# A two-layer Fourier and attention kernel: late Fourier matmuls and early score maxima as 64-row pairs, with one key tile

## The chip, the cores and the metric

The kernel runs on one core of one Trainium2 chip. The metric is the device time of one execution in microseconds. PE is TensorE (PEld its weight loads), DVE VectorE, ACT ScalarE, POOL GpSimd, SP SyncE, which issues most DMAs. A matmul's result goes to PSUM, which has eight banks of 512 fp32 columns on 128 partitions.

## The reference, cut to what matters

```python
def _A_ref(x, dft_seq_re, dft_seq_im, dft_hid_re, dft_hid_im):
    a = jnp.einsum("bsd,ed->bse", x, dft_hid_re)
    b = jnp.einsum("bsd,ed->bse", x, dft_hid_im)
    return jnp.einsum("ts,bse->bte", dft_seq_re, a) - jnp.einsum("ts,bse->bte", dft_seq_im, b)

def _B_ref(x, wq, wk, wv, wo):          # 32 query heads of 16, one key and one value head
    q = (x @ wq).reshape(B, S, H, Dh).transpose(0, 2, 1, 3)
    k, v = x @ wk, x @ wv
    p = softmax(jnp.einsum("bhqd,bkd->bhqk", q, k) * Dh ** -0.5)
    o = jnp.einsum("bhqk,bkd->bhqd", p, v)
    return o.transpose(0, 2, 1, 3).reshape(B, S, H * Dh) @ wo

x = x + _A_ref(layernorm(x), ...)       # S = 2048, D = 512
x = x + _B_ref(layernorm(x), ...)
x = x + _A_ref(layernorm(x), ...)
x = x + _B_ref(layernorm(x), ...)
```

## The kernel before

Each of the two layers has a Fourier stage (`phase_a`) and an attention stage (`phase_b`). All instructions are issued in an order written out by hand; each engine takes its own in that order. Products are made of two-part fp32r numbers, a high part `...h` and a low part `...l`: `mm3` (L87) issues high x high, high x low and low x high into the same PSUM bank.

**Fourier stage.** The output rows are in four blocks `tb` of 512. For each block the sequence transform comes first, once with the cosine matrix (c = 0) and once with the sine matrix (c = 1): a loop over n = 0..127, with `tb, c, s = n // 32, (n // 16) % 2, n % 16`, takes one chunk of 128 rows of the matrix, split into `ch` and `cl`. For each of the four column tiles d it adds `xnh`/`xnl` chunk s times the chunk into `z[d]`: twelve 128-row matmuls of 512 columns a chunk. The four banks of z are two two-bank tiles `x` (`pair()`, bufs 2). Chunks 112 to 127 (c = 1 of block 3) are worked in two halves of 256 columns. After the sixteenth chunk `z_split` (ACT, DVE and POOL) empties z into `zh[c]`, `zl[c]`. After c = 1 the hidden transform follows: `y_tile` for each of four row tiles, 24 matmuls into one bank `y`, then on DVE the residual add and the statistics of the next normalization, and a DMA to `mid`.

During block tb + 1, `prep_tasks` prepares block tb: normalization, four transposes, `kv` (n = 32 (tb + 1) + 6), v's transposes and four projections `q_mm` (+7 to +10), each into a bank `y`, and their stores to `qd` in DRAM. For block 3 that work stands behind the loop (the tail).

**Maxima.** The softmax needs each row's maximum over all keys. For some (query tile i, key block kb) this is done already in the Fourier stage: `EARLY` lists them with the query tile's slot, when to load it and between which times the 32 maxima are spread. Times there count 40 to a block, 32 chunks and 8 for y. Each is one matmul into a bank `y` (bufs 3) and one `reduce_max` on DVE. PE, DVE and the three banks are all that couples them to the rest.

The head pairs lie on the two halves of the partitions: rows 0 to 63 hold head g = 0, rows 64 to 127 head g = 1 of a pair `pr`. `kz[g]` holds the keys on half g and zeros on the other half, so the early maximum of one head takes all 128 rows of the query tile:

```python
def max_one(i, pr, g, c0, n, to):
    pm = bank("y")[:, :n]
    nc.tensor.matmul(pm, o.qT[i][:, pr, :], kz[g][:, c0:c0 + n], start=True, stop=True)
    nc.vector.reduce_max(to, pm, axis=AX.X)
```

The maxima and scores of the attention stage (`max_half` L354, `score` L739) use 64 rows of one half already, two heads after one another on different halves.

**Attention stage.** For each of 16 query tiles and 32 steps it makes the scores of four heads, ACT's exponentials, and the products with v. The change leaves its instructions as they are but for the name of the key tile.

`hl_tiles` gives four buffers each for `ch` and `cl`, which the query weights share (`wq_split`). `qd_zero` writes zeros from `kz[0]` into the spare rows of `qd` in DRAM, a task each at n = 20 + 2 t in layer 0, from POOL's queue.

Of the kernel before, what the change touches and what calls it, by code (L numbers as in the profile page):

```python
# [17 lines left out]
P = 128  # L18
S = 2048
# [22 lines left out]
]  # L42
KEPT = [e for e in EARLY if e[0]]
# [5 lines left out]
def fnet_mqa_kernel(ctx: ExitStack, tc: tile.TileContext, x_in, ct, dt_, wq, wkv, wo, out):  # L49
# [66 lines left out]
    def qd_zero(t):  # L116
        for g in range(2):
            nc.gpsimd.dma_start(qd[t, 64 * g + M0:64 * g + 64, :], f(kz[0][64:64 + 64 - M0, :]))
# [4 lines left out]
    def hl_tiles():  # L123
        return (sb.tile([P, 512], F32R, name="ch", bufs=4), sb.tile([P, 512], F32R, name="cl", bufs=4))
# [63 lines left out]
    def make_layer(L, src, mid, dst, last):  # L188
# [68 lines left out]
        def kv(t0, n, xth, xtl, vt=None, now=True):  # L257
# [15 lines left out]
        def kv_lo(t0, n):  # L273
            cs = slice(t0 * P, (t0 + n) * P)
            for g in range(2):
                gs = slice(64 * g + 32, 64 * g + 48)
                nc.vector.tensor_sub(kz[g][gs, cs], st["pk"][gs], f(kz[g][gs, cs]))
# [18 lines left out]
        def q_half(t0, g, xth, xtl, between=lambda: None):  # L296
            wh, wl = st["wqh", g]
            pq = pair()[:, 0, :256]
            for k in range(NK):
                ks = slice(k * P, (k + 1) * P)  # L300
                mm3(pq, wh[:, ks], wl[:, ks], xth[:, k, :], xtl[:, k, :], k == 0, k == NK - 1)
                between()
            if g == 0:
# [35 lines left out]
        def max_one(i, pr, g, c0, n, to):  # L339
            pm = bank("y")[:, :n]  # L340
            nc.tensor.matmul(pm, o.qT[i][:, pr, :], kz[g][:, c0:c0 + n], start=True, stop=True)  # L341
            nc.vector.reduce_max(to, pm, axis=AX.X)  # L342

        def max_early(e, pr, g):
# [3 lines left out]
            to = st["mxe"][:, KEPT.index(EARLY[e]), pr, g:g + 1] if i else partial(0)[:, pr, g, kb:kb + 1]  # L348
            max_one(i, pr, g, kb * 512, 512, to)

        def max_half(i, pr, g, kb):
            pm = bank("y")
            gs = slice(64 * g, 64 * g + KR)
            nc.tensor.matmul(pm, o.qT[i][gs, pr, :], kz[g][gs, kb * 512:kb * 512 + 512], start=True, stop=True)  # L354
            nc.vector.reduce_max(partial(i)[:, pr, g, kb:kb + 1], pm, axis=AX.X)  # L355
# [51 lines left out]
        def y_tile(tb, tt, zh, zl, x1, between={}):  # L407
# [3 lines left out]
            for cc in range(2):  # L411
                for k in range(NK):
                    mm3(y, zh[cc][:, k, tsl], zl[cc][:, k, tsl], dh[cc][:, k, :], dl[cc][:, k, :],
                        cc == 0 and k == 0, cc == 1 and k == NK - 1)
                    for fn in between.get(4 * cc + k, ()):
                        fn()
            nc.vector.tensor_add(x1, y, x1)
            nc.gpsimd.dma_start(mid[t], x1)
            ln_stats(x1, t)

# [109 lines left out]
        def phase_a(extra):  # L530
# [8 lines left out]
            if L == 0:  # L539
# [3 lines left out]
                for t in range(NT):  # L543
                    add(20 + 2 * t, lambda t=t: qd_zero(t))
# [6 lines left out]
            for e, (i, kb, k, n0, n1, n2) in enumerate(EARLY):  # L551
                if n0 is not None:
                    add(n0, lambda i=i, k=k: qT_load(i, k))
                for u in range(2 * NPAIR):
                    at = divmod(int(4 * (n1 + u * (n2 - n1) / (2 * NPAIR))), 4)
# [458 lines left out]
```

## Time and profile before

| | |
|---|---|
| median of 3 runs | 3690.29 us |
| lowest, highest | 3686.88, 3693.06 us |
| span of the profiled execution | 3683.8 us |
| PE, DVE, ACT, POOL busy | 99%, 77%, 64%, 25% |
| instructions | 57818 |

The span is from the first to the last instruction of the profiled execution; the page gives no other time for that execution. A line of the page's groups names source line, engine, operation, output and inputs, the shapes and the count. In the answers by window, each engine has its busy time and its count in brackets. "Idle before" with an arrow names what ended an engine's wait. PE's durations overlap, since matmuls are pipelined: what one costs in a stream is the distance of the starts.

### The profile page before, as it was taken

The numbers are of one execution on the slowest core, as the hardware profiler recorded it, in microseconds if no ns is written. First come the engines' busy times: TensorE is split into PE (matmuls) and PEld (weight loads), VectorE is DVE, ScalarE is ACT, GpSimd is POOL, SyncE is SP. The second block draws the span as 40 slices with busy tenths as digits, with TensorE's granted clock in tenths as the row PEclk, the third lists the DMA queues.
The fourth block names the chain that finished last, engine by engine and source line by source line (L and its number), as shares of the span: only waits on it lengthen the run. The fifth ranks groups of instructions, "written<-read, shape, count | busy, mean of one in ns | idle before, by whom it ended". The sixth has DMA issues, their size and how long they took to land. (4 is left out here: it accounts for less than half of the span.)

```text
span 3683.8 us, 57818 instructions
## 1 busy us (share of the span) xinstructions
PE 3632.3 (99%) x21792; PEld 1918.2 (52%) x21792; DVE 2825.1 (77%) x4857; ACT 2351.1 (64%) x2812; POOL 920.1 (25%) x1289
## 2 busy tenths in 40 slices
PE   8999999999999999999999999999999999999999
PEld 6877778633333333333377877785333333333333
DVE  6176988788888888888411879887888888888882
ACT  3322211588888888888933131216888888888888
POOL 5634333212112112211255342322101011010101
PEclk9999999999999999999999999999999999999999
DMA  5544233311111100110144242423111111001101
GB/s 171 145 136 146 69 103 92 104 34 45 39 36 34 48 25 23 34 49 23 41 133 128 98 140 72 116 82 101 34 48 35 36 45 36 25 22 47 36 22 27
DMA packets 218023, 246.79 MB, mean 67 GB/s; under 512 B 51664, under 2 KB 173584, under 8 KB 210064
## 3 DMA queue, kind: packets, MB, share of 16 engines
q1 hardware_dynamic: 204048, 225.78, 20.6%
q0 software_dynamic: 13696, 17.33, 1.7%
q8 instruction: 171, 2.80, 0.3%
q14 instruction: 108, 0.88, 0.1%
HBM read 178.77 MB, written 63.17 MB: 66 GB/s over the span
## 5 line engine op out<-in xcount | busy, mean ns | idle before, releaser
L742 ACT ACTIVATE slot<-x 128x1024 f32<-128x1024 f32 x1990 | 1938.2, 1025 | 293.6 <-PE x L739 278.7
L355 DVE TENSOR_REDUCE mxp<-y 128x1 f32<-128x512 f32 x2912 | 1829.9, 684 | 189.6 <-PE y L354 177.9
L753 PE MATMUL z<-slot,v 128*32 128x512 f32 x8192 | 1096.6, 605 | 2.1 <-DVE row L757 1.3
L739 PE MATMUL x<-slot,kz 64*128 64x512 f32 x2956 | 675.3, 451 | 6.2 <-DMA slot<-mt 4.8
L342 DVE TENSOR_REDUCE mxe<-y 128x1 f32<-128x512 f32 x960 | 592.4, 682 | 98.1 <-PE y L341 96.8
L739 PEld LDWEIGHTS x<-slot,kz 64*128 64x128 f32 x2956 | 278.2, 184 | 746.2 <-ACT slot L742 675.7
L354 PE MATMUL y<-kz,slot 64*128 64x512 f32 x2144 | 576.0, 396 | 4.2 <-DVE mxp L355 3.5
L88 PE MATMUL x<-ch,xnh 128*128 128x512 f32 (+1 forms) x1152 | 431.6, 375 | 13.6 <-ACT ch L79 8.6
L89 PE MATMUL x<-cl,xnh 128*128 128x512 f32 (+1 forms) x1152 | 428.0, 372 | 1.2 <-DVE cl L80 0.6
L90 PE MATMUL x<-ch,xnl 128*128 128x512 f32 (+1 forms) x1152 | 427.0, 371 | 1.5 <-POOL xnl L472 1.2
L341 PE MATMUL y<-kz,slot 128*128 128x512 f32 (+1 forms) x1216 | 414.5, 403 | 13.9 <-DVE mxe L342 7.9
L79 ACT CAST ch<-craw 128x512 fp32r<-128x512 f32 x256 | 155.2, 619 | 373.6 <-PE x L90 335.7
L80 POOL TENSOR_TENSOR cl<-craw,ch 128x512 fp32r<-128x512 f32 x236 | 305.4, 1302 | 324.3 <-ACT ch L79 296.1
L753 PEld LDWEIGHTS z<-slot,v 128*32 128x32 f32 x8192 | 164.1, 108 | 359.3 <-issue 327.9
L341 PEld LDWEIGHTS y<-kz,slot 128*128 128x128 f32 x1216 | 227.1, 188 | 121.3 <-DVE mxe L342 68.6
L354 PEld LDWEIGHTS y<-kz,slot 64*128 64x128 f32 x2144 | 274.1, 186 | 30.5 <-DVE mxp L355 17.4
L392 POOL DMA_DIRECT2D slot<-mt x208 | 102.8, 502 | 612.9 <-PE y L354 506.9
L88 PEld LDWEIGHTS x<-ch,xnh 128*128 128x128 f32 x1152 | 218.1, 189 | 46.2 <-ACT ch L79 9.4
L90 PEld LDWEIGHTS x<-ch,xnl 128*128 128x128 f32 x1152 | 217.7, 189 | 44.4 <-POOL xnl L472 4.1
L89 PEld LDWEIGHTS x<-cl,xnh 128*128 128x128 f32 x1152 | 217.4, 189 | 44.8 <-POOL cl L80 1.3
L794 POOL TENSOR_TENSOR row<-row,row 128x256 f32<-128x256 f32 x63 | 46.4, 737 | 681.7 <-DMA row<-rd 681.4
L342 DVE TENSOR_REDUCE mxp<-y 128x1 f32<-128x512 f32 (+1 forms) x256 | 144.7, 617 | 38.4 <-PE y L341 37.4
(154 smaller groups left out, 2805.5 us busy)
## 6 DMA issues: line engine op xcount, KB each, us to landing
craw<-ct_in SPq DMA_DIRECT2D x112, 512.0 KB
slot<-qd SPq DMA_DIRECT2D x48, 1024.0 KB
qd<-row SPq DMA_DIRECT2D x144, 128.0 KB
od<-row SPq DMA_DIRECT2D x252, 64.0 KB
row<-x_in SPq DMA_DIRECT2D x32, 256.0 KB
mid<-row POOLq DMA_DIRECT2D x32, 256.0 KB, 2.3
craw<-ct_in SPq DMA_DIRECT2D x32, 256.0 KB
row<-mid SPq DMA_DIRECT2D x32, 256.0 KB
```

Source lines behind the costliest of these rows:

```text
L79: nc.scalar.copy(hi, raw)
L80: (eng or nc.vector).tensor_sub(lo, raw, f(hi))
L88: nc.tensor.matmul(ps_, ah, bh, start=start, stop=False)
L89: nc.tensor.matmul(ps_, ah, bl, start=False, stop=False)
L90: nc.tensor.matmul(ps_, al, bh, start=False, stop=stop)
L341: nc.tensor.matmul(pm, o.qT[i][:, pr, :], kz[g][:, c0:c0 + n], start=True, stop=True)
L342: nc.vector.reduce_max(to, pm, axis=AX.X)
L354: nc.tensor.matmul(pm, o.qT[i][gs, pr, :], kz[g][gs, kb * 512:kb * 512 + 512], start=True, stop=True)
L355: nc.vector.reduce_max(partial(i)[:, pr, g, kb:kb + 1], pm, axis=AX.X)
L739: nc.tensor.matmul(st["e"][:, g, :], kz[g][64 * g:64 * g + KR, c * P:(c + 1) * P], o.qT[i][64 * g:64 * g + KR, cp:cp + 4, :], start=True, ...
L742: nc.scalar.activation(ptiles[i, s_][:, 2 * w:2 * w + 2, :], st.pop("e"), AF.Exp, scale=DH ** -0.5)
L753: nc.tensor.matmul(a[32 * j:32 * j + 32, :], v1[:, c, :], pt[:, j, :], start=c == 0, stop=c == NT - 1)
```

## The change

- **One key tile.** `kz` is one tile with the keys on both halves; `kv` writes it with one ACT instruction. Its first rows give `qd_zero` its zeros, until the keys of the first block overwrite them, and `qd_zero` moves to n = 4 + 2 t.
- **Early maxima as pairs.** `max_of` takes 64 rows of half g; the two heads of a pair are issued together at one point, half as many points.
- **Late Fourier matmuls as 64-row pairs.** From n = `ROWS` = 48 on, `z_rows` takes two chunks together (four half-width ones from n = 112) and issues each 128-row matmul as two 64-row ones, for two banks at a time: half 0 for one bank, half 1 for the other. In the first two of four passes q half 0 works for banks 0, then 2, half 1 for 1, then 3; in the last two they swap, in the reverse order of matmuls. The next two chunks begin with the banks as they stand.
- **Swap.** Between the passes of one pair of banks ACT copies one column per bank of the last `xnl` chunk onto itself (`relay`), so the swapped matmuls, which read it first, wait for ACT, and ACT for PE's matmuls before.
- **y and the last projections likewise.** `y_rows` makes two row tiles together in an `x` pair, both halves, with a swap; `q_rows` two projections of rows 14 and 15. Blocks 1 and 2 use it for all four tiles, block 3 for the last two; block 0 and the first two tiles of block 3 keep `y_tile`.
- **Around it.** `ch`, `cl` have six buffers; two chunks are split at a time; the tail is in another order: both last tiles end together, the two normalizations are one, and the transpose of tile 15 comes behind the last projection of rows 12 and 13.

```diff
+ROWS = 48
...
-    kz = [sb.tile([P, S], F32R, name=f"kz{g}") for g in range(2)]
-    for g in range(2):
-        nc.gpsimd.memset(f(kz[g][64 * (1 - g):64 * (1 - g) + 64, :]), 0.0)
+    kz = sb.tile([P, S], F32R, name="kz")
+    nc.gpsimd.memset(f(kz[:64 - M0, :]), 0.0)
...
-            for g in range(2):
-                gs = slice(64 * g, 64 * g + 64)
-                nc.scalar.activation(kz[g][gs, cs], pk[gs], AF.Identity, scale=kmask[gs], bias=kone[gs])
+            nc.scalar.activation(kz[:, cs], pk, AF.Identity, scale=kmask, bias=kone)
...
+        def q_rows(t0, g0, xth, xtl, after):
+            pq = pair()
+            for h in range(2):
+                for k in range(NK)[::1 - 2 * h]:
+                    ks = slice(k * P, (k + 1) * P)
+                    for u in (0, 1, 2)[::1 - 2 * h]:
+                        for g in range(2):
+                            gs = slice(64 * g, 64 * g + 64)
+                            wh, wl = st["wqh", g0 + (g ^ h)]
+                            a, b = ((wh, xth), (wh, xtl), (wl, xth))[u]
+                            nc.tensor.matmul(pq[:, g ^ h, :256], a[gs, ks], b[gs, k, :],
+                                             start=(h, k, u) == (0, 0, 0), stop=(h, k, u) == (1, 0, 0))
+                    after()
+                if h == 0:
+                    relay(xth[:, NK - 1, :1])
+            for e in range(2):
+                q_split(t0, g0 + e, pq[:, e, :256])
...
+        def max_of(i, pr, g, c0, n, to):
             pm = bank("y")[:, :n]
-            nc.tensor.matmul(pm, o.qT[i][:, pr, :], kz[g][:, c0:c0 + n], start=True, stop=True)
+            gs = slice(64 * g, 64 * g + KR)
+            nc.tensor.matmul(pm, o.qT[i][gs, pr, :], kz[gs, c0:c0 + n], start=True, stop=True)
             nc.vector.reduce_max(to, pm, axis=AX.X)
...
+        def relay(ap):
+            nc.scalar.copy(ap, f(ap))
+
+        def y_rows(tb, pairs, zh, zl, x1, after):
+            ys = [pair() for _ in pairs]
+            at = 0
+            for h in range(2):
+                for w, y in zip(pairs, ys):
+                    for cc, k in [(c, k) for c in range(2) for k in range(NK)][::1 - 2 * h]:
+                        for u in (0, 1, 2)[::1 - 2 * h]:
+                            a, b = ((zh, dh), (zh, dl), (zl, dh))[u]
+                            for g in range(2):
+                                gs = slice(64 * g, 64 * g + 64)
+                                tt = w[g ^ h]
+                                nc.tensor.matmul(y[:, g ^ h, :], a[cc][gs, k, tt * P:(tt + 1) * P], b[cc][gs, k, :],
+                                                 start=(h, cc, k, u) == (0, 0, 0, 0), stop=(h, cc, k, u) == (1, 0, 0, 0))
+                        for fn in after.get(at, ()):
+                            fn()
+                        at += 1
+                    if h == 0:
+                        relay(zl[1][:, NK - 1, w[0] * P:(w[0] + 2) * P].rearrange("p (a b) -> p a b", a=2)[:, :, :1])
+                    else:
+                        for e in range(2):
+                            y_out(4 * tb + w[e], y[:, e, :], x1[w[e]])
...
-                    add(20 + 2 * t, lambda t=t: qd_zero(t))
+                    add(4 + 2 * t, lambda t=t: qd_zero(t))
...
+            def z_rows(z, odd, chunks, first, last, split):
+                order = [(j, u) for j in range(len(chunks)) for u in range(3)]
+                for q in range(NK):
+                    for e, (j, u) in enumerate(order[::-1] if q > 1 else order):
+                        s, ch, cl = chunks[j]
+                        a, b = ((xnh, ch), (xnh, cl), (xnl, ch))[u]
+                        for g in range(2):
+                            d = ((0, 2, 1, 3), (1, 3, 0, 2))[g ^ odd][q]
+                            gs = slice(64 * g, 64 * g + 64)
+                            nc.tensor.matmul(z[d], a[gs, s, d * P:(d + 1) * P], b[gs, :],
+                                             start=first and q < 2 and e == 0, stop=last and q > 1 and e == len(order) - 1)
+                        if 2 * e + 2 == len(order):
+                            yield
+                    if q < 2:
+                        relay(xnl[:, chunks[-1][0], 256 * q:256 * q + 256].rearrange("p (a b) -> p a b", a=2)[:, :, :1])
+                    elif last:
+                        split(2 * q - 3)
+                    yield
...
-                c_split(n + 2)
+                if n < ROWS:
+                    c_split(n + 2)
+                elif n % 2 == 0:
+                    c_split(n + 2)
+                    c_split(n + 3)
...
-                    for tt in range(4):
-                        y_tile(tb, tt, zh, zl, x1[tt], {k: inner.pop(("y", tb, 8 * tt + k), ()) for k in range(8)})
+                    if n < ROWS:
+                        for tt in range(4):
+                            y_tile(tb, tt, zh, zl, x1[tt])
+                    else:
+                        y_rows(tb, ((0, 1), (2, 3)), zh, zl, x1, {k: inner.pop(("y", tb, k), ()) for k in range(32)})
...
+            y_rows(3, ((2, 3),), zh, zl, x1, {k: [lambda: take(ma, 2)] for k in (1, 3, 5, 7, 8, 10)})
+            root(14, 2)
             qT_load(1)
             o.loaded.add(1)
+            q_half(12, 0, *xt[0])
+            ln_inv(*st["root"])
+            apply(14)
+            q_half(12, 1, *xt[0])
+            apply(15)
+            q_half_store(12, 0)
+            q_half(12, 2, *xt[0])
+            tr(14)
+            q_half_store(12, 1)
+            q_half(12, 3, *xt[0])
+            tr(15)
             kv(14, 2, *xt[1], vt[0][:, 256:])
+            q_rows(14, 0, *xt[1], lambda: take(mb, 2))
+            v_tr(12, 4, vt[0])
             max_neg(0, 0, HALF, 5)
+            q_rows(14, 2, *xt[1], lambda: None)
             max_rows_pe(0, 0, HALF)
```

More of the change, by code (lines that the diff above doesn't have):

```diff
@@ L123, in hl_tiles @@
     def hl_tiles():
-        return (sb.tile([P, 512], F32R, name="ch", bufs=4), sb.tile([P, 512], F32R, name="cl", bufs=4))
+        return (sb.tile([P, 512], F32R, name="ch", bufs=6), sb.tile([P, 512], F32R, name="cl", bufs=6))
     wkvh = sb.tile([P, NK, P], F32R, name="wkvh")
@@ L416, in y_tile, with y_out @@
                         fn()
+            y_out(t, y, x1)
+        def y_out(t, y, x1):
             nc.vector.tensor_add(x1, y, x1)
@@ L623, in phase_a @@
             for n in range(125, 128):
-                for d in range(0 if n > 125 else 2, NK):
-                    inner[n, d] = [lambda: take(ma, 1)]
+                for d in (0, 2):
+                    inner[n, d] = [lambda: take(ma, 2)]
             add(124, lambda: wq_all(0))
@@ L652, in phase_a @@
                     else:
[L653 to L662 removed]
+                        next(rows)
                     for fn in inner.pop((n, d), ()):
```

83 lines of the change are left out of this document (35 added, 48 removed).

## The prediction

> **What bounds the kernel now.** I read the page first: engine shares and slices.
>
> ```profile
> PE 3632.3 (99%) x21792; PEld 1918.2 (52%) x21792; DVE 2825.1 (77%) x4857; ACT 2351.1 (64%) x2812; POOL 920.1 (25%) x1289
> DVE  6176988788888888888411879887888888888882
> POOL 5634333212112112211255342322101011010101
> ```
>
> PE looks full everywhere. The slices tell more: DVE is at 7 to 9 tenths in the second half of both Fourier stages (slices 4 to 7 and 24 to 27). The change touches those stages alone, so I cut layer 1's into stretches (the last row is layer 0's n 48-63).
>
> ```profile
> core 0: us, PE busy (x) PEld busy (x) DVE busy (x) ACT busy (x) POOL busy (x), PEclk, DMA share, GB/s
> 2025.20:2093.30 68.10, 67.96 (x291) 54.42 (x292) 61.52 (x99) 13.62 (x23) 23.41 (x19) 1.00 0.36 126
> 2093.30:2119.10 25.80, 25.80 (x113) 21.03 (x112) 15.14 (x25) 3.70 (x7) 6.45 (x7) 1.00 0.08 31
> 2119.10:2178.00 58.90, 58.68 (x259) 45.97 (x259) 35.19 (x57) 18.76 (x33) 29.43 (x27) 1.00 0.49 143
> 2178.00:2276.50 98.50, 97.13 (x403) 69.30 (x402) 97.15 (x163) 17.50 (x29) 30.74 (x24) 1.00 0.34 110
> 2276.50:2318.40 41.90, 40.46 (x161) 27.87 (x160) 37.59 (x60) 5.29 (x9) 6.75 (x7) 1.00 0.13 47
> 2318.40:2356.30 37.90, 37.05 (x166) 28.12 (x164) 33.32 (x58) 10.95 (x19) 16.72 (x17) 1.00 0.38 131
> 2356.30:2462.70 106.40, 104.19 (x529) 83.79 (x529) 86.06 (x145) 21.87 (x39) 33.77 (x27) 1.00 0.36 97
> 2462.70:2484.20 21.50, 20.87 (x153) 19.48 (x153) 19.72 (x33) 4.07 (x8) 7.66 (x10) 1.00 0.17 62
> 2484.20:2526.60 42.40, 41.44 (x290) 37.41 (x288) 23.09 (x60) 14.70 (x36) 13.41 (x18) 1.00 0.20 57
> 192.00:263.90 71.90, 69.58 (x292) 55.60 (x293) 61.71 (x99) 13.73 (x23) 25.40 (x23) 0.98 0.44 145
> ```
>
> The stretches are cut at the first matmul of a chunk n or of a y: n 48-63; y of block 1; n 64-74; n 75-94; n 95 with y of block 2; n 96-102; n 103-119 with two y tiles; n 120-124; the tail. In n 75-94 DVE is busy 97.15 of 98.50 us: it is the bound there.
>
> The prices come from the timeline: two 128-row matmuls and the load between them, two 64-row pairs, the first and last of twelve 256-column matmuls, and a run of the early maxima's reductions.
>
> ```profile
> 500.15 0.39 PE L88 MATMUL x<-ch,xnh 128*128 128x512 f32 x1
> 500.15 0.19 PEld L89 LDWEIGHTS x<-cl,xnh 128*128 128x128 f32 x1
> 500.38 0.40 PE L89 MATMUL x<-cl,xnh 128*128 128x512 f32 x1
> ```
>
> ```profile
> 1201.40 0.40 PE L354 MATMUL y<-kz,xnl 64*128 64x512 f32 x2
> 1201.63 0.41 PE L739 MATMUL x<-slot,kz 64*128 64x512 f32 x2
> ```
>
> ```profile
> 653.43 0.28 PE L88 MATMUL x<-ch,xnh 128*128 128x256 f32 x1
> ...
> 654.72 0.28 PE L90 MATMUL x<-ch,xnl 128*128 128x256 f32 x1
> ```
>
> ```profile
> 584.31 32.37 DVE L342 TENSOR_REDUCE mxe<-y 128x1 f32<-128x512 f32 x54
> ```
>
> Start to start a 128-row matmul costs 0.23 us and a pair also 0.23; 256 columns cost 1.29/11 = 0.117; a reduction costs 32.37/54 = 0.60.
>
> **The change, part by part.** *Fourier matmuls as pairs*: two 64-row matmuls for one of 128 rows at the same 0.23 a pair: nothing gained, nothing lost. *Early maxima*: two matmuls (0.46) become one pair (0.23), 0.115 saved per maximum, but only down to DVE's 0.60 per reduction. Each stretch becomes the larger of PE's new sum and DVE's.
>
> n 48-63: 99 DVE instructions, nearly all reductions, x 0.60 = 59.4; PE 192 matmuls (16 chunks of 12) and 50 pairs x 0.231 = 56. The pairs come at uneven gaps and only three banks stand between, so between 59.4 and today's 68.1 I take the middle, 63.8: **+4.3**. Layer 0's row of the same chunks is 3.8 longer; PE waits there once for the first query tile:
>
> ```profile
> PE y L341 <- DMA slot<-qd: 2.3, 1, 2.3
> ```
>
> ```profile
> L118 POOL DMA_DIRECT2D qd<-kz x32 | 16.6, 521 | 0.0
> ```
>
> These 32 DMAs of zeros (n 20-50 of layer 0 only) now leave in n 4-34, off the queues at that load. I credit **+3**, once (bounds 0 and 3.8). Moved, they cost POOL 0.52 each between the splits of the first chunks; POOL is half free there (its slices 0 to 3 read 5, 6, 3, 4), so I cost them at nothing, 1 us if it were not.
>
> y of block 1: 113 - 96 = 17 maxima x 0.115, **+1.9**. n 64-70: two a chunk by the table, 14, **+1.6**. n 75-94: **0**.
>
> n 95 and y of block 2: today a running y tile takes one of the three banks that maxima need. With y in the x pairs all three are free: by the table 6 + 44 reductions x 0.60 = 30.0, the ends of two tiles 3.1 (below), start 0.4: 33.5 against 41.9: **+8.4** before the bubbles. n 96-98, 12 maxima outside DVE's limit: **+1.4**.
>
> The projection chunks:
>
> ```profile
> 2373.91 4.88 DVE L342 TENSOR_REDUCE mxe<-y 128x1 f32<-128x512 f32 x8 [2.82 <-PE y L341]
> 2381.65 4.88 DVE L342 TENSOR_REDUCE mxe<-y 128x1 f32<-128x512 f32 x8 [2.86 <-PE y L341]
> ```
>
> One chunk is 7.74 us: 4.88 of reductions and 2.86 in which DVE idles through the q projection. That matmul group needs a bank of the same three, free only when the sixth reduction ends, 1.2 us before the eighth; 2.8 us of q, 0.7 of z and 0.4 to the first result give 2.7 again. **0** in n 71-74 and n 102-106, though DVE is free a third of the time. n 107-119 goes at DVE's rate, eight a chunk: 0. n 120-124: DVE 19.7 of 21.5, less a little for gaps: **+1.5**.
>
> *Costs.* At a tile's end DVE does an add, statistics and their sum; a Fourier bank of the second half leaves through ACT:
>
> ```profile
> 2508.55 0.69 DVE L417 TENSOR_TENSOR row<-y,row 128x512 f32<-128x512 f32 x1 [1.17 <-PE y L90]
> 2509.28 0.69 DVE L136 BATCH_NORM_STATS2 bst<-row 128x6 f32<-128x512 f32 x1
> 2510.01 0.18 DVE L137 BATCH_NORM_AGGREGATE mv<-bst 128x2 f32<-128x6 f32 x1
> ```
>
> ```profile
> L84 ACT CAST slot<-row 128x512 fp32r<-128x512 f32 x64 | 39.7, 621 | 2.4
> ```
>
> Two tile ends are 2 x 1.56 = 3.1. y now starts in the x pair that z has just filled: a hand-over of 0.4 and three ACT steps of 0.6 make 2.2 us until it is free, against 1.4 (six pairs) of cover: -0.9, after both blocks. The next z's second pair waits for two adds and the statistics between: 0.4 + 0.69 + 0.87 + 0.69 = 2.7 against 1.6: -1.1 after block 1; with up to three reductions queued ahead on DVE -2.5 after block 2.
>
> *Row modes.* Transposes, k/v and q projections keep 128 rows among 64-row pairs. The nearest case is v's 32-row transposes:
>
> ```profile
> 526.40 0.43 PE L282 MATMUL z<-ident,row 32*128 32x32 f32 x4
> 526.76 0.50 PE L88 MATMUL x<-ch,xnh 128*128 128x512 f32 x1
> 527.10 0.40 PE L89 MATMUL x<-cl,xnh 128*128 128x512 f32 x1
> ```
>
> The second matmul after it comes 0.34 later, not 0.23: 0.1 a switch, 0.2 an excursion; the four transposes in n 64-69 and a few others show: -0.8 and -0.3, the rest falls into DVE's waits (bounds: 0 to 26 excursions x 0.2 = 5 us a layer).
>
> *Swap.* Every two chunks ACT rewrites a column twice:
>
> ```profile
> 635.42 0.20 ACT L143 ACTIVATE lnw<-lnv 128x2 f32<-128x2 f32 x1 [11.85 <-DVE lnv L142]
> ```
>
> PE's drain 0.16, the copy 0.2 and two hand-overs of 0.1 make 0.55; the other bank pair's six pairs (1.4) cover it, also behind two splits (L84's price each) queued before it on ACT. If that cover is gone, see the rivals. A k/v store in one ACT instruction instead of two helps nobody but the tail.
>
> *The tail.* Both last tiles now end together, so row tile 14 is ready later:
>
> ```profile
> 2505.06 0.15 DVE L142 TENSOR_SCALAR lnv<-mv 128x1 f32<-128x1 f32 x1
> 2506.84 0.55 DVE L183 TENSOR_SCALAR row<-row,mv,rs 128x512 f32<-128x512 f32 x1 [1.19 <-POOL rs L152]
> 2518.51 0.88 DVE L277 TENSOR_TENSOR kz<-y,kz 16x256 fp32r<-16x256 f32 x2 [3.20 <-ACT row L267]
> 2519.55 5.65 DVE L342 TENSOR_REDUCE mxp<-y 128x1 f32<-128x256 f32 x16 [0.16 <-PE y L341]
> ```
>
> From y's end: adds and statistics 3.4, normalization 1.8 + 0.55, hand-overs, so the transpose of row 14 at 6.2 us; a projection (12 x 0.117 = 1.4) and the transpose of row 15 to 8.5; its split (0.62 + 0.69, behind the projection's copies on ACT) was covered by a projection and now is open, so k/v runs from 10.4 to 11.8; the ACT copies and 0.88 for k's low part let the first late maximum go at 13.7; 16 reductions, back to back today already, 5.65, to 19.5; v's transposes and the last two projections with one open swap (0.5 + 2.8 + 0.55) end at 22.8. Today that is 18.3 (2526.60 less y's end, 0.2 ahead of the add at 2508.55): -4.5. The swap inside y: -0.6. Early pairs: +0.3. Together **-4.8**.
>
> Sum of a layer: 4.3 + 1.9 + 1.6 + 8.4 + 1.4 + 1.5 - 1.8 - 3.6 - 1.1 - 4.8 = 7.8. Two layers and the stall: 15.6 + 3 = **18.6 us**. The profiled span is 3683.8; the median of the runs shown is 3690.3, 6.5 more, which I keep as what lies around the span: span 3665, time **3672**.
>
> The load row above runs while a matmul on the same 128 rows is in flight. The Trainium skill, *TensorE: Matmul & The Clock Gate*, Part 3, "The mechanism", says that a weight load overlaps matmuls in flight only if its row group differs. By that rule a stream of pairs on the same two halves would show its loads: 0.23 + 0.19 = 0.42 a pair, 146 us a layer for the 768 pairs of n 48-111. The trace disagrees (0.23 with the load inside), so I give it 0.02.
>
> **The rivals.** *The swaps show (slower).* ACT runs in order, so a rewrite queued behind a split that waits for its DMA or its bank stops PE at the third bank pair. Price: 80 swaps a layer, some 32 of them in chunks at DVE's rate where PE has time to lose; 48 x 0.55 = 26 us against 7.8, so +18.6 a layer, less the 3: 3724. It decides from (7.8 + 1.5)/48 = 0.19 us a swap. For it: PE had no dependence on ACT's order inside a block before. Against: ACT is busy 110 of 501 us in the nine rows. 0.13.
>
> *Issue (slower).* A pair of 256 columns asks PE for four instructions in 0.117 us; the trace shows two in that time, and four in 0.23. At twice the time n 120-127 and the last projections (240 pairs) cost 28 us a layer more and n 112-119 (24 x 0.234 + 0.9 a chunk against DVE's 4.8) 14: 3755. It decides from 0.156 a pair. Nothing in the trace is that dense for long, for or against. 0.10.
>
> *DVE leaves nothing.* The three banks jam more than I allow: y's 8.4 and n 48-63's 4.3 halve, 6 us remain, 3684. 0.18.
>
> *The bubbles hide.* The tail's chain and the bank waits are covered after all: 11.3 a layer more, 3649. 0.07.
>
> **How the numbers follow.** The forecast has 0.50. A measurement of this kernel tells about 0.2% (7.4 us) from no change. Faster takes the forecast less its weak end (0.48) and the last rival: 0.55. Same: 0.18. Slower: the swaps, issue, the skill's rule and what spills from unknown prices: 0.27. The forecast alone spans 3655 to 3684 by the bounds above; the range given, 3649 to 3724, reaches to the bubbles' and the swaps' cases and leaves out issue and beyond.
>
> **What would show it.** Right: n 75-94 still takes 98 us in each layer; n 95 with y of block 2 about 34 to 36; 7.7 us a projection chunk; consecutive late pairs 0.23 apart, 0.117 at 256 columns; almost no wait of PE on the rewrite's line; a tail of about 47 us where 42.4 stands; no wait for the query tile in layer 0. Wrong: pairs over 0.25 apart, a wait for the rewrite of over 0.19 on average, DVE's idle between reductions growing in n 75-94, or a tail under 42.

## The result and the profile after

The changed kernel takes **3700.3 us** (median of 5 runs, 3698.3 to 3705.9) against 3686.9 for the kernel before on the same chip (5 runs, 3685.9 to 3693.1): ratio 1.0036, 95% interval 1.0024 to 1.0049. It is 0.36% slower; the forecast was 3672, 18.6 us faster. The profiled executions say the same: a span of 3697.7 us against 3683.8, so 13.9 to explain. Part of the forecast time was 6.5 us "around the span", which compared two different executions of the kernel before; for one and the same execution of the changed kernel time and span are 1.8 apart (3699.45 and 3697.7).

The engines' line of the page after:

```profile
PE 3612.1 (98%) x24672; PEld 1822.8 (49%) x24672; DVE 2817.3 (76%) x4847; ACT 2363.3 (64%) x2974; POOL 915.5 (25%) x1288
```

TensorE has 20 us less to do and the span is 14 longer: PE now waits 34 us more. Where, the stretches of layer 1 tell, cut at the same places as the prediction's rows and with the same columns: n 48-63; y of block 1; n 64-74; n 75-94; n 95 with y of block 2; n 96-102; n 103-119 with two y tiles; n 120-124; from n 125 to the transposes of the row maxima; from there to the attention's first value matmul.

```profile
2032.35:2098.31 65.96, 65.39 (x484) 43.55 (x484) 60.67 (x100) 15.43 (x40) 23.26 (x19) 1.00 0.37 134
2098.31:2122.36 24.05, 24.05 (x210) 19.64 (x211) 12.81 (x22) 4.48 (x9) 5.75 (x6) 1.00 0.06 22
2122.36:2184.12 61.76, 59.14 (x390) 41.19 (x386) 35.95 (x60) 19.55 (x44) 31.13 (x29) 1.00 0.48 141
2184.12:2283.02 98.90, 96.42 (x643) 56.01 (x644) 97.41 (x163) 18.88 (x47) 29.06 (x23) 1.00 0.34 110
2283.02:2319.20 36.18, 33.63 (x269) 24.50 (x267) 33.77 (x57) 6.41 (x13) 6.21 (x6) 1.00 0.04 15
2319.20:2359.99 40.79, 36.48 (x251) 24.74 (x247) 35.82 (x62) 11.54 (x26) 16.98 (x19) 1.00 0.50 168
2359.99:2467.62 107.63, 103.69 (x830) 75.05 (x828) 85.80 (x144) 23.00 (x54) 33.36 (x27) 1.00 0.34 91
2467.62:2490.33 22.71, 21.73 (x285) 19.61 (x284) 18.71 (x33) 5.58 (x15) 8.88 (x11) 1.00 0.18 59
2490.33:2537.55 47.22, 41.19 (x442) 34.76 (x441) 22.99 (x55) 12.21 (x33) 11.43 (x16) 1.00 0.18 51
2537.55:2547.01 9.46, 6.43 (x23) 3.32 (x21) 6.45 (x11) 6.03 (x10) 2.88 (x6) 0.70 0.42 129
```

For the last two, the kernel before, cut at the same instructions:

```profile
2484.20:2526.31 42.11, 41.15 (x288) 37.24 (x286) 23.09 (x60) 14.44 (x35) 13.41 (x18) 1.00 0.20 57
2526.31:2533.67 7.36, 6.73 (x21) 3.26 (x21) 6.23 (x11) 5.11 (x8) 2.12 (x5) 0.77 0.46 143
```

Against the lines of before (us, after less before; the forecast is the sum of the prediction's terms in that stretch):

| stretch of layer 1 | change | forecast |
|---|---|---|
| n 48-63 | -2.1 | -4.3 |
| y of block 1 | -1.8 | -1.0 |
| n 64-74 | +2.9 | +0.6 |
| n 75-94 | +0.4 | 0 |
| n 95 and y of block 2 | -5.7 | -7.5 |
| n 96-102 | +2.9 | +1.1 |
| n 103-119 | +1.2 | 0 |
| n 120-124 | +1.2 | -1.5 |
| n 125 to the row maxima's transposes | +5.1 | +4.8 |
| from there to the first value matmul | +2.1 | 0 |
| sum | +6.2 | -7.8 |

The stages with 64-row matmuls were to win 12.6 a layer ahead of the tail, and win 1.0. The tail loses what was forecast, and 2.1 more behind its last transposes. Layer 0 has the same pattern, less the query tile's stall and with two stretches at half clock, which the last section shows.

Almost every sign that the prediction named for being right is there: n 75-94 takes 98.9 us, n 95 with y of block 2 takes 36, the tail 47.2, a projection chunk 7.9, the query tile's wait is gone, and PE hardly waits for a rewrite. Of the waits of PE in the whole run (us in total, times, longest):

```profile
PE y L361 <- DVE mxe L362: 20.8, 20, 2.6
PE y L361 <- DVE mxp L362: 10.8, 22, 1.5
...
PE x L650 <- DVE row L438: 4.2, 2, 2.1
...
PE x L456 <- ACT slot L443: 0.6, 2, 0.3
PE x L313 <- ACT xnh L443: 0.6, 2, 0.3
```

L443 is the one-column rewrite. The 160 rewrites of the Fourier matmuls (L650) are in no line of the waits; the 1.2 us fall to the 14 of the row tiles (L456) and of the projections (L313). So the swap is free, as forecast. L361 is a maximum's matmul, waiting for a bank that VectorE (L362) has still to reduce. L650 is the next block's Fourier stage, which waits for the residual add (L438) that frees its bank. The longest of these waits in layer 1 stand in TensorE's timeline (idle before, in brackets), with what VectorE did meanwhile:

```profile
2126.03 0.49 PE L650 MATMUL x<-ch,xnh 64*128 64x512 f32 x2 [2.11 <-DVE row L438]
2314.07 0.50 PE L361 MATMUL y<-kz,slot 64*128 64x512 f32 x1 [2.55 <-DVE mxe L362]
2323.84 0.50 PE L361 MATMUL y<-kz,slot 64*128 64x512 f32 x1 [2.62 <-DVE mxe L362]
```

```profile
2310.25 0.68 DVE L438 TENSOR_TENSOR row<-x,row 128x512 f32<-128x512 f32 x1
2310.97 0.69 DVE L136 BATCH_NORM_STATS2 bst<-row 128x6 f32<-128x512 f32 x1
2311.70 0.18 DVE L137 BATCH_NORM_AGGREGATE mv<-bst 128x2 f32<-128x6 f32 x1
2311.81 0.69 DVE L438 TENSOR_TENSOR row<-x,row 128x512 f32<-128x512 f32 x1
2312.53 0.69 DVE L136 BATCH_NORM_STATS2 bst<-row 128x6 f32<-128x512 f32 x1
2313.26 0.18 DVE L137 BATCH_NORM_AGGREGATE mv<-bst 128x2 f32<-128x6 f32 x1
2313.36 2.45 DVE L362 TENSOR_REDUCE mxe<-y 128x1 f32<-128x512 f32 x4
```

Two row tiles that end together put 3.1 us of adds and statistics on VectorE in one piece, with reductions queued behind; TensorE has filled the three banks by then and stands still for 2.6. Before, the tiles ended one at a time, and no wait of over 0.7 us stood in these places.

### The profile page after: what moved, and what is told of

The parts are those of the page before. It is cut to its first block, busy times and chain, and to the rows that moved or that the text cites. A ratio compares the mean times of both kernels' runs of the same rounds, so it can differ in the third digit from the quotient of the medians.

```text
span 3697.7 us, 63649 instructions
## 1 busy us (share of the span) xinstructions
PE 3612.1 (98%) x24672; PEld 1822.8 (49%) x24672; DVE 2817.3 (76%) x4847; ACT 2363.3 (64%) x2974; POOL 915.5 (25%) x1288
## 4 chain that ended last, share of the span: by engine, by line
PE 90%; DVE 6%; ACT 2%; issue 1%; POOL 1%; DMA 0%; SPq 0%; ACTq 0%; DVEq 0%; POOLq 0%
PE z L831 27%; PE y L361 18%; PE x L817 18%; PE x L650 9%; PE x L456 3%; DVE mxe L362 3%; PE y L89 3%; PE y L91 2%; PE y L90 2%; PE x L91 2%; PE x L90 2%; PE x L89 2%; DVE mxp L362 1%; ACT slot L820 1%; DVE row L183 0%
## 5 line engine op out<-in xcount | busy, mean ns | idle before, releaser
L362 DVE TENSOR_REDUCE mxp<-y 128x1 f32<-128x512 f32 (+1 forms) x3168 | 1972.0, 679 | 229.1 <-PE y L361 208.0
L361 PE MATMUL y<-kz,slot 64*128 64x512 f32 (+1 forms) x3360 | 1043.2, 407 | 36.5 <-DVE mxe L362 20.8
L362 DVE TENSOR_REDUCE mxe<-y 128x1 f32<-128x512 f32 x960 | 584.3, 682 | 96.2 <-PE y L361 89.2
L361 PEld LDWEIGHTS y<-kz,slot 64*128 64x128 f32 x3360 | 484.5, 185 | 236.0 <-DVE mxe L362 166.3
L650 PE MATMUL x<-ch,xnh 64*128 64x512 f32 (+1 forms) x1536 | 411.6, 371 | 5.6 <-DVE row L438 4.2
L650 PE MATMUL x<-ch,xnl 64*128 64x512 f32 (+1 forms) x1536 | 411.3, 371 | 0.0
L650 PE MATMUL x<-cl,xnh 64*128 64x512 f32 (+1 forms) x1536 | 391.4, 354 | 0.0
L443 ACT CAST xnl<-xnl 128x2 fp32r<-128x2 f32 x160 | 31.2, 195 | 473.6 <-PE x L650 276.4
L650 PEld LDWEIGHTS x<-cl,xnh 64*128 64x128 f32 x1536 | 248.8, 185 | 19.3
L650 PEld LDWEIGHTS x<-ch,xnh 64*128 64x128 f32 x1536 | 233.9, 185 | 28.8 <-issue 6.6
L650 PEld LDWEIGHTS x<-ch,xnl 64*128 64x128 f32 x1536 | 234.3, 185 | 19.5 <-issue 4.5
L872 POOL TENSOR_TENSOR row<-row,row 128x256 f32<-128x256 f32 x63 | 46.6, 739 | 686.2 <-DMA row<-rd 661.9
L80 ACT CAST ch<-craw 128x512 fp32r<-128x512 f32 x256 | 147.8, 618 | 39.5 <-DMA craw<-ct_in 13.9
L89 PE MATMUL x<-ch,xnh 128*128 128x512 f32 x384 | 154.8, 403 | 12.2 <-ACT ch L80 9.0
```

Of the source, the lines that this page charges most:

```text
L80: nc.scalar.copy(hi, raw)
L89: nc.tensor.matmul(ps_, ah, bh, start=start, stop=False)
L361: nc.tensor.matmul(pm, o.qT[i][gs, pr, :], kz[gs, c0:c0 + n], start=True, stop=True)
L650: nc.tensor.matmul(z[d], a[gs, s, d * P:(d + 1) * P], b[gs, :], start=first and q < 2 and e == 0, stop=last and q > 1 and e == len(order) - 1)
```

## The experiments

Each run stands beside runs of the kernel before on the same chip; the changed kernel's 3700.3 is compared through them.

**The old tail.** The last two row tiles one after the other, the last projections in single banks:

```diff
-            y_rows(3, ((2, 3),), zh, zl, x1, {k: [lambda: take(ma, 2)] for k in (1, 3, 5, 7, 8, 10)})
+            y_tile(3, 2, zh, zl, x1[2], {k: [lambda: take(ma, 2)] for k in (1, 4)})
+            root(14, 1)
+            one = {1: [lambda: ln_inv(*st["root"])], 4: [lambda: apply(14)]}
+            y_tile(3, 3, zh, zl, x1[3], one)
...
-            q_rows(14, 0, *xt[1], lambda: take(mb, 2))
+            for g in range(3):
+                q_half(14, g, *xt[1], lambda: take(mb, 2 if g else 0))
...
```

> The changed kernel with the tail of the kernel before: the last two row tiles one after the other, the q projections in single banks, the maxima of 64 rows in pairs kept. Theory (the loss is in the tail): from the first matmul of the last two row tiles to the attention's first value matmul the changed kernel's trace has 45.6 us a layer, the one before 38.2. Put back, 7.4 a layer comes back, less what the switches of row mode at the pairs cost (six pairs x 0.4): span 3697.7 - 2 x 7.4 + 2 x 2.4 = about 3688, 9 us faster than the changed kernel, at least 7. Rival (the tail only hides a wait that stands at the attention's start anyway, on ACT's queue): 0 to 4 us faster. Rival (the loss is elsewhere, in the 47 early stages): no difference.

Measured: 3687.07 (11 runs), ratio to before 1.0001, interval 0.9992 to 1.0010; span 3685.2, 12.5 below the changed kernel's (9 were expected). So the loss against the kernel before was the tail, and the attention's start did not take it back:

```profile
2482.14:2523.96 41.82, 40.85 (x345) 34.84 (x345) 22.94 (x60) 12.84 (x34) 12.20 (x17) 1.00 0.20 58
2523.96:2531.78 7.82, 6.24 (x22) 2.83 (x22) 6.37 (x11) 5.33 (x8) 2.13 (x5) 0.86 0.48 143
```

49.6 us from n 125 to the first value matmul, where the changed kernel has 56.7 and the one before 49.5. It also shows that the rest of the change, the loop with its thousands of paired matmuls, comes to nothing that can be measured: what it wins in some chunks it loses in others, as the table has it.

**The tail's two halves.** One run takes back only the paired projections of row tiles 14 and 15 (`q_rows` to `q_half`, as in the second half of the diff above), one only the paired row tiles (its first half, with the order of normalization before).

> The changed kernel with the last key tiles' q projections (row tiles 14 and 15) in the form of before: four single accumulations of 128 rows in place of two pairs of 64 rows with a swap. The last two row tiles stay a pair. Theory: the 7.4 us a layer that the tail lost are two things, the pair of row tiles (3.0 + 1.6 up to the end of k/v, less 0.9 in the tiles) and the paired projections (1.6 up to the transposes of the row maxima, 2.1 from there to the first value matmul, since ACT has four copies of the last pair queued ahead). This run takes the second away: 1.6 to 3.7 a layer, 3 to 7.5 us faster than the changed kernel. Rival: the 2.1 come from the late end of the tiles, and switches of mode at the maxima (0.4 each, six of them) eat the 1.6: 0 to 1 us.

> The changed kernel with the last two row tiles one after the other as before (each ends by itself, so that the first is normalized and transposed beside the second), and the q projections of the last two key tiles still in pairs of 64 rows. Theory: this takes the other part away, 3.0 + 1.6 - 0.9 = 3.7 us a layer, less two switches of mode at the six maxima between (2 excursions x 0.4): 6 to 8 us faster than the changed kernel, and with the run on the projections it adds up to the 11 us of the old tail. Rival: the chain to the first value matmul is set by the last projections alone; then 0 to 2 us.

```profile
2491.30:2537.91 46.61, 41.83 (x393) 34.91 (x392) 22.67 (x55) 12.70 (x34) 12.15 (x17) 1.00 0.18 52
2537.91:2545.75 7.84, 6.91 (x21) 3.12 (x22) 6.37 (x11) 5.34 (x8) 2.16 (x5) 0.73 0.44 133
```

```profile
2487.40:2530.34 42.94, 40.25 (x394) 34.64 (x393) 22.95 (x60) 12.40 (x33) 11.38 (x16) 1.00 0.20 56
2530.34:2539.34 9.00, 6.81 (x24) 3.27 (x22) 6.46 (x11) 6.03 (x10) 2.83 (x6) 0.73 0.44 129
```

With single projections (the first fence) the stretch before the transposes keeps 46.6 of the changed kernel's 47.2, and the one behind falls from 9.5 to 7.8. With the tiles apart (the second) the first falls to 42.9 and the second keeps 9.0. So the paired row tiles cost 4.3 a layer ahead of the transposes, the paired projections 0.6 there and 1.6 behind. On ScalarE, after (idle before in brackets):

```profile
2537.71 0.37 ACT L328 COPY row<-x 128x256 f32<-128x256 f32 x1 [1.78 <-PE x L313]
2538.12 0.41 ACT L329 CAST slot<-row 128x256 fp32r<-128x256 f32 x1
2538.43 0.37 ACT L328 COPY row<-x 128x256 f32<-128x256 f32 x1
2538.82 0.41 ACT L329 CAST slot<-row 128x256 fp32r<-128x256 f32 x1
2539.14 0.25 ACT L418 COPY craw<-y 32x128 f32<-32x128 f32 x1
```

And before:

```profile
2526.11 0.37 ACT L309 COPY row<-x 128x256 f32<-128x256 f32 x1 [0.92 <-PE x L90]
2526.52 0.41 ACT L310 CAST slot<-row 128x256 fp32r<-128x256 f32 x1
2526.83 0.25 ACT L400 COPY craw<-y 32x128 f32<-32x128 f32 x1
```

The copy of the transposed maxima (L418; L400 in the kernel before), for which the attention waits, stands behind four copies of two projections that ended together; before, it stood behind two. In time: tiles apart 3693.15, ratio 1.0015 (1.0006 to 1.0024), some 7 us better, as expected. Single projections 3700.49, ratio 1.0036 (1.0023 to 1.0048): no better, where 3 to 7.5 were expected. The span is 1.8 shorter. Layer 1 wins 2.2 behind n 125, and in this execution it loses 1.6 and 1.5 to stretches at half clock at n 64 and n 96. So the gain stands in the trace and is not shown in the time. In layer 1's stretches the two halves add up to what the old tail gives (2.2 and 4.7 of 7.0); in the times they do not (0 and 7 of 13).

**The price of a switch of rows.** The kernel before with one key tile and maxima in pairs of 64 rows, all Fourier matmuls still on 128 rows (the zeros leave early here too):

```diff
+            gs = slice(64 * g, 64 * g + KR)
-            nc.tensor.matmul(pm, o.qT[i][:, pr, :], kz[g][:, c0:c0 + n], start=True, stop=True)
+            nc.tensor.matmul(pm, o.qT[i][gs, pr, :], kz[gs, c0:c0 + n], start=True, stop=True)
```

> The kernel before with one key tile and the maxima as pairs of 64 rows, but all Fourier matmuls on 128 rows: each pair of maxima is an excursion from 128 rows to 64 and back. Two 128-row maxima cost 0.46 us, a pair 0.23. Theory (an excursion costs 0.4 us, as the changed kernel's intervals of 0.32 and 0.34 around its transposes say): a pair is 0.63, 0.17 more than two maxima of 128 rows, and some 190 pairs a layer of which about a third lie where DVE sets the time: 2 x 125 x 0.17 = 42 us slower than the kernel before, 20 at least. Rival (0.2 an excursion, as the prediction had it): a pair is 0.43 against 0.46, within 5 us of the kernel before.

Measured: 3783.13, ratio 1.0260 (1.0246 to 1.0274), 95 us slower. TensorE in chunk 76:

```profile
2244.54 0.50 PE L88 MATMUL x<-ch,xnh 128*128 128x512 f32 x1
2244.87 0.40 PE L89 MATMUL x<-cl,xnh 128*128 128x512 f32 x1
2245.11 0.39 PE L90 MATMUL x<-ch,xnl 128*128 128x512 f32 x1
2245.43 0.50 PE L339 MATMUL y<-kz,slot 64*128 64x512 f32 x2
2245.86 0.50 PE L88 MATMUL x<-ch,xnh 128*128 128x512 f32 x1
```

Three matmuls and a pair take 1.32 us; at 0.23 each they would be 0.92: **0.40 an excursion**, 0.1 in the interval into the pair, 0.2 in the one back and 0.1 behind it. At both switches the weight load starts only with its matmul (2245.43 and 2245.86); inside the 128-row stream it runs ahead (the load for 2245.11 starts at 2244.88). The expected price holds. The total is over twice the 42 expected, for two reasons: the trace has some 300 such excursions a layer, not 190, and few of them hide (2 x 300 x 0.17 is 102). Even the chunks that VectorE paced turn to TensorE's pace:

```profile
2244.50:2342.60 98.10, 97.31 (x365) 49.06 (x363) 95.06 (x149) 14.59 (x25) 25.64 (x20) 1.00 0.28 98
```

Chunks 76 to 93 took 88.9 us before. An estimate of TensorE's need here is 216 x 0.231 + 74.5 x 0.63 = 96.8. So the 64-row Fourier matmuls do buy something: without them the pairs of maxima cost 95 us, with them (old tail) nothing.

**The zeros.** The kernel before with the DMAs of zeros moved, `add(20 + 2 * t, ...)` to `add(4 + 2 * t, ...)`:

> The kernel before with one edit of the change: the 16 pairs of DMAs of zeros leave in chunks 4 to 34 of layer 0 instead of 20 to 50. Theory (these DMAs delay the first query tile at chunk 48): the wait of 2.3 us is gone, n 48 is 3.7 us shorter in layer 0, and POOL's issues between the splits of the first chunks cost 1 to 2.2 us: 1.5 to 2.7 us faster. Rival (the wait has another cause): chunk 48 keeps its wait and the early chunks add up to 2 us: 0 to 2 us slower.

Measured: 3686.98, ratio 0.9998 (0.9989 to 1.0007); span 3683.1 against 3683.8. The trace bears the theory out: PE's wait for the query tile is gone, chunks 48 and 49 of layer 0 take 8.9 us instead of 12.6, and the first 32 chunks take 2.0 longer. So the prediction's +3 is some 1.7 net: it put nothing, 1 at most, for these issues on POOL. The time can't tell 1.5 from nothing.

**Adds first.** In the paired row tiles, both residual adds ahead of the statistics:

```diff
-                            y_out(4 * tb + w[e], y[:, e, :], x1[w[e]])
+                            nc.vector.tensor_add(x1[w[e]], y[:, e, :], x1[w[e]])
+                        for e in range(2):
+                            nc.gpsimd.dma_start(mid[4 * tb + w[e]], x1[w[e]])
+                            ln_stats(x1[w[e]], 4 * tb + w[e])
```

> The changed kernel with one edit: at the end of two row tiles both residual adds go ahead of the statistics, so that the banks are free one statistic earlier. Theory (the next matmuls into these banks, of the next block's Fourier stage or of the q projections in the tail, wait for the second add): 0.69 + 0.18 = 0.87 us at up to three places a layer, of which the last row tiles' is on the path for certain: 1.7 to 5 us faster than the changed kernel. Rival (they wait for something else): no difference.

```profile
PE x L653 <- DVE row L465: 1.2, 1, 1.2
```

The wait for the second add in layer 1 falls from 2.1 to 1.2, by the 0.87 expected. The time, 3697.94 and 1.0027 (1.0017 to 1.0038), lies within the intervals of the changed kernel's: in the direction expected, not proved.

**Spreading the maxima.** The loop's gain is held back where maxima stand too dense: in n 48-63 two chunks take 8.2 us where TensorE needs 5.5 and 1.4. First placing, with the old tail:

```diff
-    (0, 0, 2, 44, 56, 61.5), (1, 0, 3, 44, 61.5, 66.5), (2, 0, 2, 54, 66.5, 70.9), (3, 0, 8, 50, 70.9, 87),
-    (0, 1, 0, 66, 87, 91), (1, 1, 1, 66, 91, 94.7), (3, 1, 8, None, 94.7, 98.7),
+    (2, 0, 2, 44, 56, 63), (1, 0, 3, 44, 63, 69.8), (3, 0, 8, 50, 69.8, 82), (0, 0, 0, 64, 82, 87),
+    (0, 1, 0, None, 87, 91), (1, 1, 1, 66, 91, 94.7), (3, 1, 8, None, 94.7, 98.7),
```

> The changed kernel with the old tail and a new placing of the first four query tiles' maxima: 32 pairs instead of 48 in chunks 48 to 63, the third tile in block 1's second stage and the first five chunks of block 2, the fourth (read from another buffer, loaded at chunk 64) in chunks 66 to 70. Theory: in chunks 48 to 63 the pairs come near the rate that VectorE can take (8.2 us for two chunks, where 24 Fourier pairs x 0.231 = 5.5); with 2.1 pairs a chunk TensorE sets the time, 5.5 + 4.3 x 0.23 = 6.5, 1.6 less in each of 7.5 steps = 12; the 16 pairs moved cost 0.23 each where TensorE is the bound already, 3.7: 8 us a layer, 16 in all, span 3669. Rival (chunks 48 to 63 are paced by the splits or loads of the stream, not by VectorE): below 5 us in all.

Measured: 3685.03, ratio 0.9994 (0.9985 to 1.0003). Chunks 48 to 61 win 8.6 a layer (12 were expected up to chunk 62), so VectorE, and not the stream's loads, held them back; chunks 66 to 71 lose 9.2 where 3.7 were expected. No gain over the old tail is shown.

```profile
2118.27 0.64 PE L361 MATMUL y<-kz,slot 64*128 64x512 f32 x1 [1.56 <-DVE mxp L362]
```

A maximum there waited 1.56 us for a bank, with the row tiles' normalizations ahead of its reduction on VectorE, and half clock followed (from 2118.48 on).

On that kernel, the q projections of blocks 1 and 2 in two halves, in the transposes' bank (`bank("z")`, two of the four k at a time):

> The kernel with the new placing, and the q projections of blocks 1 and 2 in two halves of 6 matmuls within a chunk, in the transposes' bank instead of one of the three that the maxima use. Theory: a projection chunk is 7.9 us, of which VectorE idles 2.9 behind 12 matmuls in a row; in halves the three banks cover nearly all of it, and TensorE becomes the bound: 2.77 + 0.92 + 2.77 + 0.8 (two excursions) = 7.3: 0.6 a chunk x 8, 5 us a layer, 10 in all beyond the new placing. Rival (the second excursion and ACT's copies out of the one bank take it back): between 3 us slower and 2 faster.

Measured: 3685.58, ratio 0.9995 (0.9987 to 1.0004); a pair of projection chunks takes 15.9 us, as without the halves (15.8; 15.4 in the kernel before). The rival's range held: there is a second excursion in each chunk, and VectorE still idles 1.5 us behind each half.

Second placing, on the first with the adds first: `(2, 0, 2, 44, 56, 62), (1, 0, 3, 44, 62, 68.2), (3, 0, 8, 50, 68.2, 78), (0, 0, 0, 64, 82.5, 88.5), (0, 1, 0, None, 88.5, 91.7), (1, 1, 1, 66, 91.7, 94.7)`.

> The changed kernel with the old tail, the residual adds ahead of the statistics, and the first four query tiles' maxima placed anew: 36 pairs in chunks 48 to 61 and the first stage's end, 12 in block 1's row tiles, none in chunks 64 and 65, the tile that is loaded at chunk 64 at 2.7 pairs a chunk from the middle of chunk 66 (the first placing had 3.2 there and waited 1.6 us for VectorE's normalizations, and a stretch at half clock followed). Theory: chunks 48 to 62 keep their gain (two chunks in 6.9 instead of 8.2: 8.5 us), chunks 66 to 71 lose only the moved pairs' 0.23 each and some, 4 instead of 8, the adds give 0.9 at two places: 5 to 6 us a layer, ratio to the kernel before 0.997, 3677. Rival (chunks 66 to 71 are bound by VectorE, which has the normalizations there): they lose 8 again, ratio 0.999.

Measured: 3683.36, ratio 0.9986 (0.9977 to 0.9995). Between the two, and short of the 3677 expected: chunks 48 to 61 win 7.1 and 62 to 65 win 3.9, chunks 66 to 71 lose 3.2, but 72 to 77 lose 6.4. The same placing in the kernel before:

> The kernel before with the same placing of the maxima and nothing else changed. Theory (its maxima are single matmuls of 128 rows at 0.23 each, so chunks 48 to 62 are bound by TensorE there: two chunks are 24 x 0.231 = 5.5 plus 12 x 0.24 = 8.4): the 12 pairs taken out of these chunks come back as 24 x 0.23 in later ones where TensorE is the bound too: 0 to 2 us slower a layer. So the placing pays only with the pairs. Rival (VectorE is the bound in these chunks of both kernels): 5 us a layer faster here too.

Measured: 3698.5, ratio 1.0026 (1.0016 to 1.0036), 9 us slower, where 0 to 4 were expected. Chunks 48 to 61 win 4.6 here too, which is the 20 maxima moved out of them at 0.23 each; chunks 66 to 77 lose 9.2, as the same chunks lose with the pairs (9.6). With 128-row maxima this placing costs; with the pairs it comes out even or a little better (0.9986, against 1.0001 for the old tail alone), and that run has the early adds as well, so what the placing gives by itself is not shown.

Third placing, `(0, 0, 0, 64, 82.5, 87.3), (0, 1, 0, None, 87.3, 91), (1, 1, 1, 66, 91, 94.7)` in the second:

> The version with old tail, early adds and the second placing, with one change of the placing: the tile loaded at chunk 64 is used up at 3.3 pairs a chunk from the middle of chunk 66 to 71 (2.7 to 72 before), the two tiles after it keep the pace of the changed kernel. Theory: against the old tail alone the second placing wins 8.6 in chunks 48 to 62, 4 in 62 to 65, and loses 3.1 in chunks 66 to 71 and 6.4 in 72 to 77, where VectorE is the bound and 2 pairs a chunk more cost 1.2 each. Moved back ahead of chunk 71, some 4 pairs cost 0.23 to 0.6 in place of 1.2: 2 to 4 us a layer, 3677 to 3680, ratio to the kernel before 0.997 to 0.998. Rival (the normalizations on VectorE in chunks 66 and 67 stall TensorE again, as in the first placing, with a stretch at half clock): no better than the second placing, 0.9985 or more.

Measured: **3681.08**, ratio 0.9981 (0.9972 to 0.9990): 7 us faster than the kernel before and 19 faster than the changed one, the version that beats both. It joins three edits, the old tail, the early adds and the placing. 3677 to 3680 was expected; the intervals of the second and third placing overlap, so that the third is better than the second is not shown. Its chunks 48 to 61, and the changed kernel's:

```profile
2022.63:2072.94 50.31, 49.93 (x407) 37.89 (x409) 44.12 (x71) 13.30 (x34) 22.36 (x18) 1.00 0.38 139
```

```profile
2032.35:2089.79 57.44, 57.08 (x426) 38.25 (x427) 53.79 (x89) 13.30 (x34) 22.79 (x18) 1.00 0.40 144
```

VectorE is relieved from 53.8 of 57.4 us to 44.1 of 50.3, and TensorE sets the pace: 7.1 us. Some 18 of 89 maxima went elsewhere for that, 2.1 of TensorE's time at 0.115. Chunks 62 to 65 win 3.9 more and 66 to 71 lose 7.6, so n 48 to 109 as a whole gains 2.4.

## Why the prediction was wrong, step by step

**What held.** A pair of 64-row matmuls costs 0.23 us and 0.117 at 256 columns, so issue is no bound; the swap is hidden; n 75-94 stays VectorE's; the query tile's stall goes (though the moved DMAs take over half of that back). The rivals of the swaps, of issue and of the weight loads are out. The tail's chain was read rightly: 4.8 forecast, 5.1 measured, nearly all of it in the paired row tiles as its working said.

**What failed: the terms ahead of the tail**, 12.6 forecast a layer, 1.0 measured. Three terms were mis-sized, and one behind the tail was left out.

*The switch of rows.* The prediction took 0.2 an excursion from the second interval behind a transpose and let only five or so show, 1.1 a layer. It is 0.40: the interval into the other mode and the one back count too. The transposes of row tiles in n 66-68, at a place where nothing waits, show nearly as much: 0.1 in the interval into them, 0.59 us for the four where the kernel before has 0.35 (2128.93 to 2129.28 in its trace), and 0.34 behind them where it has 0.32, 0.36 together:

```profile
2133.58 0.40 PE L361 MATMUL y<-kz,slot 64*128 64x512 f32 x2
2133.91 0.66 PE L250 MATMUL z<-ident,row 128*128 128x128 f32 x4
2134.50 0.49 PE L650 MATMUL x<-ch,xnl 64*128 64x512 f32 x1
```

The trace has 24 excursions between n 64 and n 125 of layer 1, 9.6 us if all of them show, in just the stretches that lost: n 64-74, n 96-102, n 103-119 and n 120-124 lose 8 together where 0.2 was forecast. An estimate for two of them: in n 64-74 six excursions at 0.40, four projection chunks that go from 7.74 to 7.9, and the wait of 2.1, less the 1.6 credited to the maxima, make +3.5, and +2.9 was measured; in n 96-102 six excursions and a wait of 2.6, less 1.4, make +3.6, and +2.9 was measured. So outside the projection chunks most excursions show; no run separates them from the waits. The Trainium skill, *TensorEngine Tiling (Array Packing)*, section "Tiling Modes", says that a change of mode drains the engine and gives no price. The runs fit that: the loads do not run ahead across a switch, and the price is 0.40 an excursion.

*The bubbles.* After y of block 1 the wait is 2.1, not 1.1: a pair of reductions, the first add and its statistics stood ahead of the second add. Around y of block 2 there are two waits of 2.6, not one of 2.5: the middle of the stage, where the first two tiles end, was left out.

*The rate of maxima.* n 48-63 was put at the middle between VectorE's sum and the old time, 4.3; it gave 2.1, for VectorE works 60.7 of 66.0 us and the bursts leave TensorE waiting. That the density of the placing held it back, the three placings show: 7 to 8.6 us in the same chunks. In n 120-124 the +1.5 did not come either: three excursions make 1.2 there, and two waits for a bank 0.9. The rival "DVE leaves nothing" named this; it halved this term and y's, and of the two only the first came out so (n 95 and y of block 2: 5.7 of 7.5).

*Behind the tail.* The sum ended at the last projections. Two projections that end together queue four copies on ScalarE ahead of the copy that the attention waits for: 2.1 a layer, 1.6 of it gone with single projections.

The rival "the bubbles hide" was refuted. No rival said what happened: nearly all mechanisms as described, several of them a microsecond or two dearer at each place. The bound of 5 us on the switches (26 x 0.2) was a bound on the count, with the price taken for certain; with 0.4 it would have been 10, and with all of them showing the forecast near no change.

## What to carry to other kernels

When the gain is a sum of many small terms and the loss another, price the commonest small cost from all the intervals that it touches, in and out, and multiply by the count before waving it into "waits that are there anyway". Pairing work so that two results end together doubles what lands at once on the engine behind: look at the next consumer's queue at each such place (VectorE behind two row tiles, ScalarE behind two projections), and pair only where nobody waits for the first result. A faster TensorE may pay only after the other engine's work is spread to match: here the change with its old tail was worth nothing, and it gained 7 us with the reductions moved out of the dense chunks and the adds first; a placing of that kind without the change cost 9 us.

## What the runs showed of the hardware

**Half clock after short waits.** The granted clock falls to half for 3.4 us (or twice that) after some of the new waits. In layer 0 of the changed kernel it did so behind the 2.1 us wait at n 64:

```profile
283.59:288.60 5.01, 2.90 (x26) 2.06 (x24) 4.23 (x8) 0.19 (x1) 1.62 (x3) 1.00 0.14 52
288.60:292.00 3.40, 3.40 (x20) 2.66 (x18) 1.54 (x4) 1.21 (x4) 2.38 (x4) 0.50 0.39 102
```

It did so again within y of block 2, 2.0 us into the wait of 2.55. The same waits in layer 1 had none, and in each run they fall elsewhere. What differs is where a wait lies. Within each trace all stretches at half clock begin a whole multiple of 3.413 us apart, so the time can be cut into pieces of that length. In layer 0 the 2.11 us of idle at n 64 lie in one piece (285.14 to 288.55); in layer 1 the same 2.11 are split over two, 1.01 and 1.10, and no half clock followed; with single projections they lie in one again (2121.71 to 2125.12), and it followed. In the 13 traces, from 30 us on, each of the 38 pieces at full clock with over 1.9 us of idle on TensorE was followed by half clock, and 10 of the 69 with 1.2 to 1.9 were. So a wait of 2 us costs some 1.6 more (chunks 64 and 65 take 9.97 us against 8.42) or nothing, by where it falls. This may have hidden the gains of the runs with single projections and early adds; that it did is not shown. The Trainium skill, *TensorE: Matmul & The Clock Gate*, section "HAM oscillation — how this bites in real kernels", gives the rule of no idle gaps over some 3.4 us. Keeping to it was not enough here: waits of 2.1 and 2.5 us were followed by half clock, and in the first placing one of 1.6.

**The switch between 128 and 64 rows** costs 0.40 us an excursion, there and back, with 512 columns at 0.23 a matmul, and 0.36 around four transposes.
